# Sink-window attention and a SoLU layer on one core: the probabilities of chunks 8 to 22 turned by block DMAs through DRAM and 32x32 transposes on VectorE, with all steps in a new order

## The chip, the core and the metric

The kernel runs on one core of a Trainium2 chip. The metric is the device time of one execution in microseconds (us). Engines are named as in the profile: PE (TensorE, with PEld for its weight loads), DVE (VectorE), ACT (ScalarE), POOL (GpSimd) and SP (SyncE, which issues all DMAs here).

## The reference

Causal attention with a window of 128 positions and 4 sink positions that every query sees, for 4 batches of 8 heads, 768 positions and 64 columns a head. Its output goes, token by token, through a layer of 512 to 1024 to 512 columns with a SoLU and a layer norm between the two matrices.

```python
def _attn_ref(q, k, v, n_sink, window):          # 4 x 8 x 768 x 64
    scores = q @ k.T / sqrt(64)                  # kept where j < n_sink or 0 <= i - j < window
    a = exp(scores - max) / (sum + 1e-9)
    return a @ v

def _moe_ref(x, w_in, w_out, g_ln):              # x: 3072 x 512
    h = x @ w_in                                 # 512 -> 1024
    solu = h * softmax(h)
    ln = (solu - mean) / sqrt(var + 1e-6) * g_ln
    return ln @ w_out                            # 1024 -> 512
```

## The kernel before

The 3072 tokens are 24 chunks of 128 (4 batches of 6), numbered 0 to 23 in the order of work: 0 and 1 are the first blocks of batches 0 and 1, 2 to 6 and 7 to 11 the rest of these two batches, 12 to 17 batch 2, 18 to 23 batch 3. Chunks 12 and 18 are therefore first blocks of their batch.

A chunk passes these steps, each a small function of the kernel. `score` makes the scores of one head by two matmuls (L640, L641) into one of two PSUM banks. A bank holds the keys of this block and of the block before; `pick` (DVE, L647) chooses at each column whichever of the two is inside the window. `mask` (DVE, L658) adds the mask, takes the row maximum and frees the bank. `exps` (ACT, L669) makes exponentials and their sums, `invert` (DVE) the reciprocal of a sum, `normalise` (POOL, L680) multiplies, for half of the heads (`hb` is 0 or 1, four heads each). The probabilities `sc` stand with queries on partitions, and the product with v wants keys there. `turn_p` (PE, L687) transposes the four heads of a half into a PSUM tile `ptp`, and `take_p` (ACT, L691) copies this to `pt` in SBUF. `part_new` and `part_old` (POOL, L696, L702) split `pt` into keys of this block and of the one before, by the triangle. The sink columns go another way (`sinks_hi`, `sinks_lo`, `turn_sinks`, tiles `sk`, `skp`, `skt`). `value` (PE, L740, L751) multiplies by v into `av`: this is the PV step. Then `hidden` (PE, L771) makes 1024 columns `h` with three matmuls for one product (high and low halves), the SoLU and the norm follow on DVE, ACT and POOL, and for chunks 2 to 21 the result `u` is turned without PE: `store_u` writes it to DRAM (`ud`, L818), four `load_u` read it back with its 32-row blocks moved (`ub`, L823), and `flip_u` (DVE, L828) transposes each 32x32 block. `project` (PE, L858) multiplies by the second matrix into `o`, again three matmuls for one product, and `store` writes the output.

Every engine runs its instructions in order. The order is written out by hand: `ORDER` is a list of step numbers, and the kernel calls the steps one after another as it says. Tiles come from pools with few buffers: two banks for scores, three buffers for `sc`, three for `pt`, three for the tag `u` (which `u` and `ub` share), two for the tag `ob` (the output tile).

Of the kernel before, what the change touches and what calls it, by code (L numbers as in the profile page):

```python
# [19 lines left out]
    345, 0, 142, 2, 4, 143, 5, 243, 12, 347, 349, 59, 68, 6, 50, 350, 352, 7, 41, 23, 8, 146, 153, 244, 351, 145, 154,  # L20
    247, 3, 9, 147, 60, 254, 61, 62, 10, 155, 165, 181, 69, 161, 177, 70, 166, 182, 344, 156, 255, 164, 186, 180, 86,
    51, 71, 162, 178, 184, 163, 179, 72, 159, 185, 160, 52, 53, 54, 11, 74, 32, 24, 448, 42, 175, 176, 353, 183, 63,
    14, 25, 188, 26, 73, 75, 246, 76, 77, 65, 100, 157, 248, 348, 43, 56, 27, 190, 355, 93, 44, 45, 87, 64, 357, 66,
    144, 262, 278, 67, 29, 88, 107, 263, 279, 33, 89, 34, 35, 47, 28, 30, 261, 31, 277, 356, 360, 359, 452, 15, 55,
    57, 192, 36, 38, 90, 449, 16, 58, 17, 18, 267, 358, 187, 78, 459, 128, 283, 79, 80, 46, 48, 285, 189, 260, 276,
    49, 363, 101, 37, 94, 39, 81, 284, 354, 264, 135, 371, 102, 121, 40, 280, 191, 95, 20, 288, 96, 266, 282, 97, 19,
    194, 245, 103, 193, 21, 114, 104, 108, 265, 281, 109, 22, 207, 290, 83, 208, 82, 84, 1, 379, 464, 209, 552, 98,
    85, 256, 292, 364, 110, 111, 99, 129, 130, 287, 294, 131, 361, 286, 289, 214, 215, 216, 372, 450, 369, 380, 460,
    377, 136, 137, 210, 258, 112, 211, 386, 212, 362, 365, 370, 138, 378, 385, 291, 217, 346, 115, 373, 657, 381, 213,
    293, 218, 462, 366, 374, 389, 295, 382, 368, 376, 384, 391, 219, 308, 451, 309, 453, 454, 393, 220, 367, 310, 311,  # L30
    312, 315, 375, 461, 316, 387, 317, 456, 458, 91, 383, 388, 463, 455, 401, 457, 556, 139, 116, 390, 405, 760, 470,
    656, 403, 222, 117, 313, 395, 563, 478, 314, 761, 392, 553, 394, 402, 404, 92, 118, 397, 223, 406, 486, 465, 119,
    228, 407, 469, 399, 762, 473, 396, 398, 318, 408, 477, 481, 485, 319, 140, 105, 467, 471, 400, 409, 479, 320, 475,
    487, 483, 132, 410, 227, 321, 564, 411, 472, 226, 480, 225, 555, 412, 229, 113, 558, 557, 488, 230, 491, 560, 559,
    492, 416, 417, 468, 106, 413, 414, 122, 494, 123, 466, 415, 554, 474, 323, 231, 562, 482, 561, 565, 566, 257, 496,
    506, 418, 476, 322, 419, 489, 498, 484, 124, 567, 500, 764, 490, 125, 660, 667, 233, 126, 866, 120, 493, 495, 141,
    232, 505, 864, 234, 575, 235, 507, 236, 771, 583, 508, 497, 499, 237, 501, 867, 420, 329, 510, 591, 324, 569, 503,
    511, 328, 326, 571, 577, 502, 327, 512, 585, 330, 421, 579, 573, 587, 865, 127, 422, 504, 513, 668, 238, 514, 581,
    515, 589, 133, 134, 659, 520, 521, 221, 224, 332, 662, 661, 669, 663, 671, 331, 664, 516, 517, 576, 666, 518, 424,
    584, 425, 592, 570, 665, 670, 574, 334, 578, 582, 586, 590, 595, 239, 572, 240, 1078, 596, 580, 588, 519, 1086,  # L40
    423, 1087, 594, 427, 598, 593, 430, 333, 428, 600, 675, 522, 610, 683, 691, 241, 674, 682, 676, 684, 690, 523,
    602, 612, 597, 599, 429, 604, 692, 679, 687, 335, 609, 606, 695, 763, 524, 677, 608, 601, 685, 336, 765, 693, 611,
    337, 658, 767, 673, 681, 614, 615, 603, 605, 607, 1088, 431, 338, 698, 766, 768, 339, 325, 689, 616, 871, 868,
    525, 678, 680, 686, 694, 688, 697, 773, 527, 617, 770, 772, 775, 769, 526, 699, 618, 340, 341, 433, 619, 624, 774,
    528, 696, 700, 531, 701, 703, 620, 342, 621, 435, 780, 713, 702, 704, 432, 434, 436, 788, 625, 869, 796, 626, 779,
    787, 795, 714, 1089, 870, 532, 705, 715, 706, 778, 786, 622, 716, 718, 874, 707, 709, 708, 426, 627, 777, 623,
    711, 794, 719, 535, 533, 785, 793, 802, 710, 628, 1180, 529, 782, 790, 798, 781, 789, 712, 801, 720, 721, 629,
    797, 630, 438, 784, 722, 783, 437, 534, 882, 1189, 242, 439, 440, 872, 873, 883, 884, 441, 723, 724, 632, 635,
    975, 875, 728, 729, 730, 791, 799, 886, 877, 1188, 879, 631, 977, 792, 800, 442, 979, 443, 876, 537, 1190, 931,
    804, 981, 1191, 805, 803, 636, 731, 633, 888, 725, 536, 726, 806, 807, 896, 817, 1192, 885, 538, 727, 808, 444,  # L50
    878, 880, 819, 904, 637, 445, 818, 890, 889, 638, 1282, 446, 540, 639, 820, 809, 810, 811, 976, 812, 822, 897,
    898, 906, 814, 542, 813, 543, 544, 891, 815, 823, 545, 905, 824, 1384, 887, 732, 912, 816, 825, 539, 541, 733,
    899, 907, 546, 343, 826, 1382, 734, 895, 903, 1179, 1076, 827, 911, 915, 892, 900, 978, 917, 894, 547, 984, 735,
    828, 986, 548, 919, 641, 736, 737, 902, 910, 908, 739, 893, 832, 829, 640, 985, 927, 901, 992, 909, 914, 980, 833,
    982, 830, 913, 916, 987, 740, 1385, 831, 642, 742, 990, 918, 998, 643, 1181, 834, 835, 530, 743, 920, 922, 1000,
    644, 646, 647, 836, 447, 1006, 645, 837, 991, 999, 928, 921, 1383, 1007, 549, 550, 634, 924, 929, 648, 838, 930,
    649, 926, 1008, 932, 989, 933, 997, 923, 1005, 840, 843, 925, 650, 741, 1013, 993, 1001, 1009, 934, 935, 1077,
    1014, 1017, 1080, 651, 1082, 1290, 1084, 936, 995, 652, 1003, 1019, 1029, 841, 839, 994, 1011, 1002, 1010, 996,
    1004, 847, 937, 1079, 653, 1081, 1021, 1023, 1090, 845, 551, 1031, 1015, 938, 1183, 1012, 846, 1281, 942, 943,
    738, 744, 844, 1025, 1016, 1018, 1083, 1095, 1096, 1104, 1103, 1389, 1111, 944, 654, 746, 748, 1020, 974, 945,  # L60
    849, 1030, 1032, 1280, 1291, 1292, 1112, 1185, 1117, 1027, 939, 940, 941, 1098, 1022, 946, 1034, 1035, 947, 1097,
    1106, 1114, 1392, 750, 751, 1105, 1387, 1024, 1026, 745, 752, 753, 1113, 1092, 1036, 948, 747, 749, 1028, 1037,
    1100, 950, 1108, 951, 754, 1094, 1093, 953, 13, 1038, 1101, 1118, 848, 1039, 755, 851, 756, 757, 850, 1388, 1040,
    1041, 1293, 955, 852, 949, 1042, 1102, 1109, 758, 842, 1120, 1091, 1182, 1184, 1186, 1110, 1494, 1386, 854, 855,
    1099, 1107, 1195, 1203, 1211, 1283, 1285, 952, 1196, 1115, 1044, 1116, 956, 954, 1204, 1212, 1119, 1121, 1131,
# [90 lines left out]
P = 128  # L156
# [56 lines left out]
def _banded(ctx, tc, q, k, v, n_sink, window, w_in, w_out, g_ln, out, val, wts, wpool, consts):  # L213
# [660 lines left out]
    def loads(n):  # L874
        b, c = place(n)
        return 1 if turned(n) else 4 * (c == (b < EARLY))
# [194 lines left out]
```

## Time and profile before

| | us |
|---|---|
| runs, median of 3 (lowest to highest) | 452.35 (451.55 to 452.65) |
| the profiled execution | 452.25 |
| its span, first to last instruction | 450.3 |
| PE busy | 431.2 |
| PEld (weight loads) busy | 348.1 |
| DVE busy | 349.4 |
| ACT busy | 330.6 |
| POOL busy | 238.8 |

Busy time of an engine is the union of its instructions; weight loads overlap with matmuls. Of PE the granted clock was full (1.00, the upper of its two levels, 2.4 GHz) in all stretches but the last few us. A page lists a matmul as longer than the distance to the next, because matmuls are pipelined; how fast PE goes is read from the starts.

### The profile page before, as it was taken

Reading aid. Unit: us, or ns where it says so; the run is one execution under the profiler, and the core shown is the slowest. Engines: PE = TensorE matmul, PEld = TensorE weight load, DVE = VectorE, ACT = ScalarE, POOL = GpSimd, SP = SyncE. Lnnn points to the kernel's source line nnn. Section 1 sums busy time; section 2 is a strip of 40 time slices with the busy share of each in tenths; the row PEclk is TensorE's granted clock in tenths of the full one; section 3 lists DMA queues with packets and bytes.
Section 4 is the critical chain, followed back from the end, with each engine's and each line's share of the span. In section 5 each row is a group of like instructions: output and inputs, shape, how many; then the busy total and the mean of one; then the engine's idle time right before and its main releaser. Section 6 shows DMA issues by size and latency. Waiting matters only on the chain.

```text
span 450.3 us, 8541 instructions
## 1 busy us (share of the span) xinstructions
PE 431.2 (96%) x2631; PEld 348.1 (77%) x2631; DVE 349.4 (78%) x998; ACT 330.6 (73%) x843; POOL 238.8 (53%) x369
## 2 busy tenths in 40 slices
PE   4979899999999999999999999999999999999995
PEld 3536677888888788888888888877878878888884
DVE  2999999887997897887978797786878787767140
ACT  5989898888858865888797787686687865665442
POOL 7742455668667562667635775465536266344200
PEclk9999999999999999999999999999999999999999
DMA  8999287999899899635569997946815324242001
GB/s 226 280 342 265 47 165 107 127 175 183 209 155 166 203 183 176 176 95 144 118 174 175 192 165 141 172 143 166 199 26 186 117 71 146 90 141 70 25 26 52
DMA packets 142759, 67.74 MB, mean 150 GB/s; under 512 B 118956, under 2 KB 129460, under 8 KB 142708
## 3 DMA queue, kind: packets, MB, share of 16 engines
q1 hardware_dynamic: 142708, 67.13, 67.2%
q8 instruction: 23, 0.38, 0.4%
q14 instruction: 28, 0.23, 0.2%
HBM read 38.80 MB, written 16.91 MB: 124 GB/s over the span
## 4 chain that ended last, share of the span: by engine, by line
PE 65%; DVE 15%; ACT 7%; issue 4%; POOL 3%; DMA 3%; SPq 2%; POOLq 0%; DVEq 0%; ACTq 0%
PE o L858 25%; PE h L771 20%; PE av L751 6%; PE bank L640 4%; PE bank L641 3%; PE ptp L687 3%; DVE wbits L418 2%; DVE wbits L413 2%; ACT sc L669 2%; POOL sc L680 2%; DVE sc L658 2%; DMA ub<-ud 1%; PE av L740 1%; DMA wraw<-in_moe_w_in_dram 1%; DVE wbits L409 1%
## 5 line engine op out<-in xcount | busy, mean ns | idle before, releaser
L680 POOL TENSOR_TENSOR sc<-sc,rs 128x544 f32<-128x544 f32 (+1 forms) x48 | 55.9, 1166 | 95.7 <-DVE rs L675 76.5
L669 ACT ACTIVATE sc<-sc,nmx 128x136 f32<-128x136 f32 (+1 forms) x192 | 76.3, 400 | 16.9 <-DVE nmx L658 16.4
L858 PE MATMUL o<-w2h,uh 128*128 128x512 f32 (+1 forms) x200 | 81.2, 406 | 0.0
L609 POOL TENSOR_TENSOR ring<-kf,ring 64x512 fp32r<-64x512 f32 x48 | 65.7, 1370 | 27.7 <-ACT ring L604 21.0
L771 PE MATMUL h<-w1h,xh 128*128 128x512 f32 x192 | 77.3, 403 | 0.0
L858 PE MATMUL o<-w2h,ul 128*128 128x512 f32 (+1 forms) x200 | 77.0, 385 | 0.0
L858 PE MATMUL o<-w2l,uh 128*128 128x512 f32 (+1 forms) x200 | 77.0, 385 | 0.0
L771 PE MATMUL h<-w1h,xl 128*128 128x512 f32 x192 | 76.3, 397 | 0.1
L771 PE MATMUL h<-w1l,xh 128*128 128x512 f32 x192 | 75.8, 395 | 0.0
L658 DVE CUSTOM_DVE_ANT_0 sc<-bank,bias 128x136 f32<-128x136 f32 (+1 forms) x192 | 55.2, 294 | 11.1 <-PE bank L641 3.3
L640 PE MATMUL bank<-ring,qT 128*128 128x264 f32 (+1 forms) x176 | 51.6, 303 | 1.8 <-DVE nmx L658 1.6
L641 PE MATMUL bank<-ring,qX 128*128 128x264 f32 (+1 forms) x176 | 48.7, 283 | 0.0
L858 PEld LDWEIGHTS o<-w2h,ul 128*128 128x128 f32 x200 | 37.6, 188 | 8.6 <-DVE ul L846 0.5
L858 PEld LDWEIGHTS o<-w2h,uh 128*128 128x128 f32 x200 | 37.6, 188 | 8.6 <-issue 3.3
L771 PEld LDWEIGHTS h<-w1h,xl 128*128 128x128 f32 x192 | 36.0, 188 | 10.5 <-DVE xl L760 1.9
L691 ACT COPY pt<-ptp 128x512 f32<-128x512 f32 x48 | 27.5, 581 | 19.0 <-PE ptp L687 18.8
L640 PEld LDWEIGHTS bank<-ring,qT 128*128 128x128 f32 x176 | 33.1, 188 | 10.7 <-DVE nmx L658 4.8
L858 PEld LDWEIGHTS o<-w2l,uh 128*128 128x128 f32 x200 | 37.7, 189 | 4.5
L771 PEld LDWEIGHTS h<-w1h,xh 128*128 128x128 f32 x192 | 36.1, 188 | 5.7
L771 PEld LDWEIGHTS h<-w1l,xh 128*128 128x128 f32 x192 | 36.1, 188 | 5.5
L696 POOL TENSOR_SCALAR_AFFINE_SELECT pc<-pt 128x512 f32<-128x512 f32 x40 | 28.0, 701 | 21.7 <-ACT pt L691 21.5
L846 DVE TENSOR_TENSOR ul<-ur,uh 128x512 fp32r<-128x512 f32 x40 | 32.0, 802 | 8.0 <-ACT uh L842 8.0
(137 smaller groups left out, 976.4 us busy)
## 6 DMA issues: line engine op xcount, KB each, us to landing
qX<-qT SPq DMA_DIRECT2D x88, 128.0 KB, 2.6
ud<-u SPq DMA_DIRECT2D x20, 512.0 KB, 3.2
ub<-ud SPq DMA_DIRECT2D x80, 128.0 KB, 2.8
vn<-in_v_dram SPq DMA_DIRECT2D x24, 256.0 KB, 4.9
out_dram<-ob SPq DMA_DIRECT2D x23, 256.0 KB, 2.8
kn<-in_k_dram SPq DMA_DIRECT2D x12, 384.0 KB, 5.4
qn<-in_q_dram SPq DMA_DIRECT2D x12, 384.0 KB, 6.0
wraw<-in_moe_w_in_dram SPq DMA_DIRECT2D x8, 512.0 KB, 6.1
```

The source lines that it names most:

```text
L609: nc.gpsimd.tensor_tensor(t[ROWS[1 - x]], src[ROWS[x]], t[ROWS[x]].bitcast(F32), op=ALU.subtract)
L640: nc.tensor.matmul(o, st["qT", n, x][:, r, :], rhs, start=True, stop=False)
L641: nc.tensor.matmul(o, st["qX", n, x][:, r, :], rhs, start=False, stop=True)
L658: nc.vector.tensor_tensor_reduce(out=st["sc", n, hb][:, j, c0:c1], in0=st["s", n, h].rearrange("p a x -> p (a x)")[:, c0:c1], in1=bias0 if ...
L669: nc.scalar.activation(sc[:, i, c0:c1], sc[:, i, c0:c1], AF.Exp, bias=nmx[:, i:i + 1], scale=-1.0, accum_out=ssum[:, i:i + 1])
L680: nc.gpsimd.tensor_tensor(sc[:, :, c0:c1], sc[:, :, c0:c1], rs.unsqueeze(2).to_broadcast([P, HB, c1 - c0]), op=ALU.mult)
L691: nc.scalar.copy(pt, st["ptp", n, hb])
L696: nc.gpsimd.affine_select(pc, st["pt", n, hb], pattern=[[0, HB], [1, P]], compare_op=ALU.is_ge, fill=0.0, base=0, channel_multiplier=-1)
L751: nc.tensor.matmul(acc[ROWS[x], r, :], vals[:, 2 * r + x, :], p[:, 2 * jp + x, :], start=alone, stop=alone or (r, i) == (NPAIR - 1, 1))
L771: nc.tensor.matmul(st["h", n][:, cols], a[:, kt, :], w[:, kt, cols], start=(kt == 0 and m == 0), stop=(kt == KT1 - 1 and m == 2))
L846: nc.vector.tensor_tensor(ul, st["utp", n, g4], st["uh", n, g4].bitcast(F32), op=ALU.subtract)
L858: nc.tensor.matmul(st["o", n, i], a[:, kt % 4, :], part(w, kt)[:, i * wide:(i + 1) * wide], start=(kt == 0 and m == 0), stop=(kt == KT2 - ...
```

## The change

For chunks 8 to 22, without the first blocks 12 and 18, `turn_p` and `take_p` are gone. `normalise` writes the probabilities (without sink columns) to a new tile `pn`, in an order with the 32-column group outermost, and normalises the sink columns in place with a second, small instruction. `store_p` writes a half to a DRAM tile `pd`; four `load_p` read it back so that each block of 32 rows lies on the partitions of its 32 columns (`pb`); `flip_p` transposes the 32x32 blocks on DVE into `pt`. From `pt` on all is as before. `pn` takes buffers of the tag `ob`, and `pb` buffers of the tag `u`. `ORDER` is a new list for the whole kernel. Two names in the diff are set elsewhere: `HB` is 4 (heads a half), `SEG` 132 (columns of a block in a bank: 4 sink columns and 128 keys).

```diff
+FIRST_P, LAST_P = 8, 22
 ORDER = (
-    345, 0, 142, 2, 4, 143, 5, 243, 12, 347, 349, 59, 68, ...
+    344, 0, 12, 4, 142, 2, 345, 5, 143, 59, 348, 68, 32, ...
+    def carried(n):
+        return FIRST_P <= n <= LAST_P and place(n)[1] > 0
     def normalise(n, hb):
         c0, c1 = cols_of(place(n)[1])
         sc, rs = st["sc", n, hb], st["rs", n, hb]
-        nc.gpsimd.tensor_tensor(sc[:, :, c0:c1], sc[:, :, c0:c1], rs.unsqueeze(2).to_broadcast([P, HB, c1 - c0]),
-                                op=ALU.mult)
+        if not carried(n):
+            nc.gpsimd.tensor_tensor(sc[:, :, c0:c1], sc[:, :, c0:c1], rs.unsqueeze(2).to_broadcast([P, HB, c1 - c0]),
+                                    op=ALU.mult)
+            return
+        pn = st["pn", n, hb] = sb.tile([P, 4, HB, 32], F32, tag="ob", name=f"pn_{n}_{hb}", bufs=2)
+        nc.gpsimd.tensor_tensor(pn.rearrange("p g h f -> p h g f"),
+                                sc[:, :, 4:SEG].rearrange("p h (g f) -> p h g f", f=32),
+                                rs.unsqueeze(2).unsqueeze(3).to_broadcast([P, HB, 4, 32]), op=ALU.mult)
+        sv = sc.rearrange("p h (g s) -> p h g s", s=4)[:, :, 0:SEG // 4 + 1:SEG // 4, :]
+        nc.gpsimd.tensor_tensor(sv, sv, rs.unsqueeze(2).unsqueeze(3).to_broadcast([P, HB, 2, 4]), op=ALU.mult)
+
+    def store_p(n, hb):
+        if ("pd", n) not in st:
+            st["pd", n] = dr.tile([P, H * P], F32, tag="pd", name=f"pd_{n}", bufs=4)
+        wide = HB * 32
+        nc.sync.dma_start(st["pd", n].rearrange("p (g x) -> p g x", g=4)[:, :, hb * wide:(hb + 1) * wide],
+                          st["pn", n, hb].rearrange("p g h f -> p g (h f)"))
+
+    def load_p(n, g):
+        if ("pb", n) not in st:
+            st["pb", n] = sb.tile([P, 4, H * 32], F32, tag="u", name=f"pb_{n}", bufs=3)
+        nc.sync.dma_start(st["pb", n][32 * g:32 * (g + 1)],
+                          st["pd", n].rearrange("(c t) (g x) -> g t c x", c=4, g=4)[g])
+
+    def flip_p(n, hb):
+        pt = st["pt", n, hb] = sb.tile([P, HB, P], F32, tag="pt", name=f"pt_{n}_{hb}", bufs=3)
+        nc.vector.transpose(pt.rearrange("p h (c t) -> p h c t", c=4),
+                            st["pb", n].rearrange("p c (h f) -> p h c f", f=32)[:, hb * HB:(hb + 1) * HB])
...
+    def kept(k):
+        return lambda n: 0 if carried(n) else k
+
+    def carries(k):
+        return lambda n: k if carried(n) else 0
...
-        rest_k: 2, ring_sinks: 1, score: H, pick: H, mask: H, exps: NPAIR, invert: NHB, normalise: NHB, turn_p: NHB,
-        take_p: NHB, part_new: NHB, ...
+        rest_k: 2, ring_sinks: 1, score: H, pick: H, mask: H, exps: NPAIR, invert: NHB, normalise: NHB, turn_p: kept(NHB),
+        take_p: kept(NHB), store_p: carries(NHB), load_p: carries(4), flip_p: carries(NHB), part_new: NHB, ...
```

What the new order does is seen at three places. PE, before, near the end of the middle part: `bank` is a score bank, `o_18` the accumulator of chunk 18's projection, `ptp_21_1` the PSUM tile of the second half of chunk 21.

```order
L640 MATMUL bank_1_90<-ring_126,qT_22_0_4731 128x264
L641 MATMUL bank_1_90<-ring_126,qX_22_0_4793 128x264
L858 MATMUL o_18_0_4893<-w2h_0_484,uh_18_0_4760 128x512
L858 MATMUL o_18_0_4893<-w2l_0_485,uh_18_0_4760 128x512
L858 MATMUL o_18_0_4893<-w2h_0_484,ul_18_0_4772 128x512
L687 MATMUL ptp_21_1_4903<-ident_91,sc_21_1_4802 128x128 x4
L858 MATMUL o_18_0_4893<-w2h_0_484,uh_18_0_4760 128x512
L858 MATMUL o_18_0_4893<-w2l_0_485,uh_18_0_4760 128x512
L858 MATMUL o_18_0_4893<-w2h_0_484,ul_18_0_4772 128x512
```

PE in the changed kernel, where the sink columns of the same chunk 21 are turned (`skp_21`), between triplets of chunk 20's hidden layer:

```order
L643 MATMUL bank_0_89<-ring_126,qT_22_0_4575 128x264
L644 MATMUL bank_0_89<-ring_126,qX_22_0_4694 128x264
L803 MATMUL h_20_4856<-w1h_62,xh_20_4798 128x512
L803 MATMUL h_20_4856<-w1l_63,xh_20_4798 128x512
L803 MATMUL h_20_4856<-w1h_62,xl_20_4827 128x512
L755 MATMUL skp_21_4899<-ident_r_96,sk_21_4840 128x128
L803 MATMUL h_20_4856<-w1h_62,xh_20_4798 128x512
L803 MATMUL h_20_4856<-w1l_63,xh_20_4798 128x512
L803 MATMUL h_20_4856<-w1h_62,xl_20_4827 128x512
```

The two groups of four transposes of a chunk stand no more among PE's matmuls; only the sink columns are turned there.

DVE, before, at the second half of chunk 10's scores (`sc_10_1`; the ISA rows are `mask`):

```order
L550 STREAM_TRANSPOSE qf_12_2446<-qn_2_2055 128x512
L647 COPY_PREDICATED bank_0_89<-m_cur_115,bank_0_89 128x128
L647 COPY_PREDICATED bank_1_90<-m_cur_115,bank_1_90 128x128
L658 ISA sc_10_1_2428,nmx_10_1_2429<-bank_1_90,bias2_114 128x136
L658 ISA nmx_10_1_2429 128x1
L658 ISA sc_10_1_2428,nmx_10_1_2429<-bank_0_89,bias2_114 128x136
L658 ISA nmx_10_1_2429 128x1
```

DVE in the changed kernel, at the same scores:

```order
L650 COPY_PREDICATED bank_1_90<-m_cur_115,bank_1_90 128x128
L661 ISA sc_10_1_2291,nmx_10_1_2292<-bank_1_90,bias2_114 128x136
L661 ISA nmx_10_1_2292 128x1
L712 STREAM_TRANSPOSE pt_9_0_2366<-pb_9_2288 128x512
L712 STREAM_TRANSPOSE pt_9_1_2378<-pb_9_2288 128x512
L650 COPY_PREDICATED bank_0_89<-m_cur_115,bank_0_89 128x128
L661 ISA sc_10_1_2291,nmx_10_1_2292<-bank_0_89,bias2_114 128x136
L661 ISA nmx_10_1_2292 128x1
```

The two flips of chunk 9, which need the four loads of `pb_9`, now stand between the release of bank 1 and that of bank 0.

SP, before, at chunk 10's swaps of q halves (`qX`; PE's scores read them):

```order
L593 DMA qX_10_0_2085<-qT_10_0_1835 64x512
L594 DMA qX_10_0_2085<-qT_10_0_1835 64x512
L509 DMA qn_2_2055<-in_q_dram 32x96x32
L818 DMA ud_7_2188<-u_7_2149 128x1024
L509 DMA qn_2_2055<-in_q_dram 32x96x32
L823 DMA ub_7_2230<-ud_7_2188 32x4x256
L593 DMA qX_10_1_2256<-qT_10_1_2253 64x512
L594 DMA qX_10_1_2256<-qT_10_1_2253 64x512
```

SP in the changed kernel, at the same swaps and behind them:

```order
L701 DMA pd_9_2192<-pn_9_0_2138 512x1x128
L512 DMA qn_2_1967<-in_q_dram 32x96x32
L596 DMA qX_10_1_2228<-qT_10_1_2144 64x512
L597 DMA qX_10_1_2228<-qT_10_1_2144 64x512
L701 DMA pd_9_2192<-pn_9_1_2225 512x1x128
L901 DMA out_0_dram<-ob_4_0_2163 128x512
L850 DMA ud_7_2254<-u_7_2247 128x1024
L707 DMA pb_9_2288<-pd_9_2192 32x4x256
L596 DMA qX_11_0_2295<-qT_11_0_2270 64x512
L597 DMA qX_11_0_2295<-qT_11_0_2270 64x512
L707 DMA pb_9_2288<-pd_9_2192 32x4x256 x3
```

The stores of a chunk's two halves and its four loads stand between the swaps and the loads of q; the swap of chunk 11 stands behind the first load of `pb_9`, which waits for the stores.

## Rows read from the trace of the kernel before

**Rows 1.** The page's first part: busy us of each engine, share, instructions.

```profile
PE 431.2 (96%) x2631; PEld 348.1 (77%) x2631; DVE 349.4 (78%) x998; ACT 330.6 (73%) x843; POOL 238.8 (53%) x369
```

**Rows 2.** Stages: busy PE, PEld, DVE, ACT, POOL; PEclk, DMA share, GB/s.

```profile
0.00:60.00 60.00, 48.18 (x216) 32.10 (x217) 49.93 (x132) 48.86 (x122) 31.78 (x58) 1.00 0.81 230
60.00:150.00 90.00, 89.31 (x578) 73.69 (x579) 79.75 (x229) 73.69 (x187) 59.43 (x85) 1.00 0.98 161
150.00:400.00 250.00, 248.92 (x1563) 204.87 (x1564) 200.48 (x595) 185.16 (x488) 137.48 (x208) 1.00 0.64 148
```

**Rows 3.** Timeline of PE, the place in the order: start, us, instruction.

```profile
378.55 0.28 PE L640 MATMUL bank<-ring,qT 128*128 128x264 f32 x1
...
378.79 0.29 PE L640 MATMUL bank<-ring,qT 128*128 128x264 f32 x1
...
379.28 0.40 PE L858 MATMUL o<-w2l,uh 128*128 128x512 f32 x1
379.51 0.40 PE L858 MATMUL o<-w2h,ul 128*128 128x512 f32 x1
379.75 0.60 PE L687 MATMUL ptp<-ident,sc 128*128 128x128 f32 x4
380.11 0.48 PE L858 MATMUL o<-w2h,uh 128*128 128x512 f32 x1
380.42 0.39 PE L858 MATMUL o<-w2l,uh 128*128 128x512 f32 x1
```

**Rows 4.** Stage, instructions on `ptp` alone: PE, PEld, ACT; then the same.

```profile
150.00:400.00 250.00, 17.82 (x120) 14.29 (x120) 17.31 (x30) 1.00 0.64 148
```

**Rows 5.** Groups by line and form: busy us, mean ns; idle before.

```profile
L691 ACT COPY pt<-ptp 128x512 f32<-128x512 f32 x48 | 27.5, 581 | 19.0 <-PE ptp L687 18.8
...
L828 DVE STREAM_TRANSPOSE ur<-ub 128x512 f32<-128x512 f32 x40 | 27.9, 700 | 0.4 <-issue 0.3
...
L718 POOL TENSOR_TENSOR sk<-sc,sk 128x32 fp32r<-128x32 f32 x40 | 12.1, 310 | 16.7 <-ACT sk L711 16.2
...
L680 POOL TENSOR_TENSOR sc<-sc,rs 128x544 f32<-128x544 f32 x40 | 46.6, 1166 | 72.7 <-DVE rs L675 57.2 <-ACT ring L604 4.3 <-ACT sc L669 3.4
...
L647 DVE COPY_PREDICATED bank<-m_cur,bank 128x128 f32<-128x128 int32 x88 | 24.9, 288 | 7.6 <-PE bank L641 7.0
...
L658 DVE CUSTOM_DVE_ANT_0 sc<-bank,bias 128x136 f32<-128x136 f32 x160 | 46.5, 296 | 7.5 <-POOL sk L718 1.1
...
L669 ACT ACTIVATE sc<-sc,nmx 128x136 f32<-128x136 f32 x160 | 63.8, 401 | 15.3 <-DVE nmx L658 14.9
...
L669 ACT ACTIVATION_READ_ACCUMULATOR sc<-sc,nmx 128x1 f32 x192 | 36.3, 189 | 0.0
...
L696 POOL TENSOR_SCALAR_AFFINE_SELECT pc<-pt 128x512 f32<-128x512 f32 x40 | 28.0, 701 | 21.7 <-ACT pt L691 21.5
```

**Rows 6.** DMA issues: count, KB each, median us to landing.

```profile
ud<-u SPq DMA_DIRECT2D x20, 512.0 KB, 3.2
...
vn<-in_v_dram SPq DMA_DIRECT2D x24, 256.0 KB, 4.9
```

**Rows 7.** Tile `ub`: issue ns min/median/max, first and last start; landing.

```profile
L823 SPq DMA_DIRECT2D ub<-ud x80: 303/430/3316, 92.1 to 405.7; - x80
...
DMA to landing us min/median/max: 2.4/2.8/6.9
```

**Rows 8.** Waits of the DMA queue: us in total, times, longest.

```profile
SPq L823 <- DMA ud<-u: 38.3, 16, 4.2
```

**Rows 9.** Stretches of 10 us, columns as in the stages.

```profile
110.00:120.00 10.00, 10.00 (x73) 8.29 (x73) 9.56 (x26) 8.40 (x18) 6.15 (x13) 1.00 1.13 195
120.00:130.00 10.00, 9.86 (x50) 8.09 (x49) 9.75 (x24) 6.38 (x20) 8.09 (x10) 1.00 0.56 157
160.00:170.00 10.00, 10.00 (x76) 8.38 (x75) 8.95 (x28) 7.01 (x15) 6.76 (x12) 1.00 1.36 182
```

**Rows 10.** Waits of DVE from 150 to 400 us: us in total, times, longest.

```profile
DVE bank L647 <- PE bank L641: 9.9, 15, 2.0
```

## What I expected

> **What bounds the kernel now.** I read the page's busy shares first: TensorE (PE) is busy 431.2 us of a 450.3 us span, VectorE (DVE) 349.4, ScalarE (ACT) 330.6, GpSimd (POOL) 238.8 [rows 1]. A mean over stages can mislead, so the table by stage comes next: from 60 to 150 us PE is busy 89.31 of 90 us and from 150 to 400 us 248.92 of 250, so all its waiting there is 1.8 us [rows 2]. Busy time alone does not prove that PE has no room, since a pipelined matmul is listed as longer than the step to the next. The starts decide that [rows 3]: two 512-column matmuls follow each other by 0.23 to 0.24 us (379.28, 379.51, 379.75), so a triplet costs 0.70 us; a pair of score matmuls costs 0.24 (378.55 to 378.79); there is no hole between. In this middle part the time is the sum of PE's steps. The first 60 us (PE busy 48.18) have other limits. The change does not touch what is turned there: of the 192 transposes into `ptp`, 120 lie between 150 and 400 us [rows 4], eight each of the 15 chunks 8 to 22.
>
> In the Trainium skill, "Perfetto Trace Analysis", section "Identifying the Most-Contended Engine", matmul busy time is called a bad measure of TensorE's headroom and weight-load time a good one. By that rule PE would have 18% to spare in the middle (204.87 us of weight loads in 250), and rival 3 would be likelier than I make it; the starts disagree.
>
> **What it removes.** Chunks 8 to 22 without 12 and 18, which open a batch, are 13 chunks of two halves: 26 groups of four transposes. One group's price is read from the starts [rows 3]: the four take 379.75 to 380.11, 0.36 us, and the matmul behind them needs 0.31 to its successor where 0.235 is usual. Together 0.435 us; 26 x 0.435 = **11.3 us**, all in the middle, where PE has no other cover for it. On ACT 26 copies out of PSUM go, 26 x 0.581 = 15.1 us [rows 5], at an engine with 185 of 250 us busy [rows 2]: worth nothing by itself.
>
> **What it adds.** (a) DVE: 26 transposes of 128x512. The trace has that instruction at 0.700 us [rows 5]: 18.2 us. (b) POOL: normalising becomes two instructions. The small one is nearest to the 128x32 subtraction at 0.310 us [rows 5], 26 x 0.31 = 8.1 us; the big one now writes runs of 32, which the trace does not show for this operation. I keep 1.166 us (its old row), with half as much again, 1.75, as the far end. POOL has 137 of 250 us busy, so both matter only for the length of the turn. (c) SyncE and the DMA engines: per chunk two stores of 256 KB in 512-byte pieces and four loads of 128 KB. The loads have the shape of the `ub` loads: 0.43 us to issue, 2.8 us to landing in the median, 2.4 at least, 6.9 at most [rows 7]. The stores lie between a `ud` store (512 KB in long pieces, 3.2 us) and a `vn` load (256 KB in short pieces, 4.9 us) [rows 6]; I take 3.2, since direction and target are the same, and keep 4.9. SyncE issues 78 more DMAs (34 us) and stands 13 more times before a load until its store has landed; 16 such waits took 38.3 us [rows 8], so some 31 us more. That is 65 us on a queue that runs in order. Queued behind such a wait are the q swaps, `ub` loads and output stores, as the SyncE piece of the order shows; PE's scores wait for the swaps.
>
> **The turn itself becomes longer.** From the last score of a chunk to its PV step: pick 0.29, mask 0.30, two exponentials of 0.401 + 0.189, normalise 1.17, splitting in two 0.701 twice [rows 5], and about 1 us for the division and the hand-overs (my estimate): 5.3 us common to both. Before, four transposes and a copy add 0.435 + 0.581: 6.4 us. Now a store 3.2, three more issues 1.3, the last landing 2.8 and one transpose 0.70 add 8.0: **13.3 us**. Does PE have that much to do meanwhile? I counted, in the orders of both kernels, its steps between those two points, at 0.70 a triplet, 0.24 a score pair and 0.435 a turn [rows 3] (PV and sink steps left out, so it is counted low). Before it was 8.4 us (chunk 22) to 14.7 (chunk 14). Now it is 14.3 (22), 14.5 (21), 15.9 (8) to 22.0 (13). The new order pays for the longer turn with a longer lead, and the slack over the need stays about the same: 1.0 to 8.7 us against 2.0 to 8.3. With the store at 4.9 us or the normalising at its far end, chunks 21 and 22 are short by less than 1 us and the others are not. Chunks 8 and 9 share the DMA engines with loads of q in short pieces: the DMA share there is 1.36, against 0.64 in the middle [rows 2, 9].
>
> **What is late next: DVE's queue.** From 150 to 400 us DVE has 200.48 busy of 250 us [rows 2]. With 18.2 more it is 218.7 of 238.7: 92%, and its idle time must shrink from 49.5 to 20 us. A flip that waits for its load holds up the masks behind it; the DVE piece of the order shows the release of a score bank right behind two flips, and PE has two such banks. Can DVE run so full? From 110 to 130 us it did: 9.56 and 9.75 of 10 us, with PE at 10.00 and 9.86 [rows 9]. And the longest of its waits in the middle is for PE's own scores, 9.9 us [rows 10]; that part goes when PE gets faster.
>
> **Sum.** Span 450.3 - 11.3 = 439.0 us. New waits on PE: between none and the 8.7 us of rival 2 I take 2.7, 0.2 us for each of 13 turns, nearest to the row of now: 1.8 us of waiting over some 20 chunks, with a slack of the same size [rows 2]. Span 441.7; the profiled run took 452.25 us for a span of 450.3, so 1.95 lie outside, and the median of the runs is 0.1 above it: **443.7 us**. The first 60 us are re-ordered too and nothing is removed there; PE's idle 11.8 us in them [rows 2] can move either way, and I keep 1 us for that.
>
> **Rivals.**
> 1. *DVE becomes the bound (slower).* Its 49.5 us of idle time in the middle are waits of an in-order queue. If they all stay, because masks and flips wait as often as before, the middle takes 200.48 + 18.2 + 49.5 = 268 us, 18 more than 250: 470 us. It decides once idle stays above 31.3 us; with 37 of the 49.5 left the middle is 255.7 and the time 458. For it: 92% where the mean was 80%. Against it: 97% over the 20 us of [rows 9]. The Trainium skill sides with it ("VectorE: DVE Perf Modes", "Rules for kernel authors"): a 128x128 transpose belongs on TensorE if its result may lie in PSUM, and a DVE transpose is best within 32x32. A group of four heads costs 0.435 us on PE and 0.70 on DVE here, so the trace agrees on the engine time; it does not say which engine is short.
> 2. *Turns come late where the DMA engines are full.* Stores and loads of chunks 8 to 11 stand behind q loads, and `ub` landings came as late as 6.9 us [rows 7]. Two landings each 2.5 us late over a slack of 2.6 to 6 us cost 1.5 us in each of these four chunks, and 0.3 in the nine others: 8.7 us. Of the gain 2.6 us stay: 449.7.
> 3. *PE has headroom after all*, so what is removed was hidden: 452, no change. Against it speak the starts in [rows 3]; only places where PE waits anyway would hide it, and those add up to 1.8 us.
> 4. *All of it and a better start*: no new waits, and 1 us from the head: 440.
>
> **Chances.** Forecast (441 to 447): 0.58. Rival 1 (around 458): 0.12. Rival 2 (447 to 452): 0.17, of which 0.13 are still a gain that can be measured. Rival 3: 0.05. Rival 4: 0.08. A measurement of this kernel tells some 0.3% (1.4 us) from no change, so faster means below 451.0: 0.58 + 0.13 + 0.08 = 0.79; same 0.04 + 0.05 = 0.09; slower 0.12. The range leaves out rivals 1 and 3 and a little at either end: 440.3 to 451.0.
>
> **What would show it.** Right: PE's busy time 11 us smaller at the same spacing of 0.235 us; PE idle from 60 us to the last chunks below 5 us; DVE at 90% or more in the middle with its flips at 0.70 us; 22 copies on ACT in place of 48. Rival 1 shows as PE waiting for masks while DVE is busy throughout or stands at a flip. Rival 2 shows as landings of the new loads well over 3 us, with DVE waiting at the flips of chunks 8 to 11. The prediction is wrong if PE's idle time after the first 60 us grows by more than 6 us, or if the first 60 us change by more than 2.

## The result and the profile after

The changed kernel takes **448.06 us** (median of 6 runs, 446.73 to 449.33) against 452.50 for the kernel before (6 runs, 451.55 to 453.09): ratio 0.9897, interval 0.9883 to 0.9911. It is faster by 4.4 us and inside the range; 8.8 were forecast, and the time misses the forecast's own band of 441 to 447. Its profiled execution took 448.04 us for a span of 446.3.

The page's first part (engines, busy us, share, instructions) and the stages, columns as in [rows 1] and [rows 2]:

```profile
PE 421.2 (94%) x2527; PEld 336.3 (75%) x2527; DVE 364.6 (82%) x1024; ACT 317.4 (71%) x817; POOL 241.9 (54%) x395
```

```profile
0.00:60.00 60.00, 46.84 (x214) 31.66 (x215) 48.06 (x133) 48.45 (x121) 31.46 (x58) 0.97 0.81 225
60.00:150.00 90.00, 86.37 (x559) 69.65 (x559) 82.25 (x228) 74.31 (x193) 57.97 (x84) 1.00 1.02 169
150.00:400.00 250.00, 247.25 (x1504) 200.93 (x1504) 217.54 (x632) 173.41 (x462) 143.19 (x234) 1.00 0.86 201
```

PE's busy time fell by 10.0 us (431.2 to 421.2), so the work did leave PE. Its idle time in the span rose by 6.0, from 19.1 to 25.1 us, and the stages say where: 11.8 to 13.2 in the first 60 us, 0.7 to 3.6 from 60 to 150, 1.1 to 2.75 from 150 to 400. More than two thirds of the new idle time lies ahead of 150 us.

Groups by line and form (busy us, mean ns; then idle before): the new instructions cost what the rows before said.

```profile
L691 POOL TENSOR_TENSOR pn<-sc,rs 128x512 f32<-128x512 f32 x26 | 29.5, 1136 | 40.1 <-ACT sc L672 19.8 <-DVE rs L678 9.5 <-ACT qT L579 3.5
...
L712 DVE STREAM_TRANSPOSE pt<-pb 128x512 f32<-128x512 f32 x26 | 17.6, 693 | 0.0
...
L695 POOL TENSOR_TENSOR sc<-sc,rs 128x32 f32<-128x32 f32 x26 | 8.5, 326 | 0.0
```

DMA issues (count, KB each, median us to landing), and the `pd` stores (issue ns min/median/max, first and last start in us):

```profile
pd<-pn SPq DMA_DIRECT2D x26, 256.0 KB, 3.0
pb<-pd SPq DMA_DIRECT2D x52, 128.0 KB, 2.9
```

```profile
L701 SPq DMA_DIRECT2D pd<-pn x26: 553/561/2730, 152.3 to 388.2; - x26
```

The first store is issued at 152.3 us. Before that moment nothing is turned through DRAM, and only the order differs.

**The new waits from 60 to 150 us.** Waits of PE in this stage (total, times, longest); together 3.4 us, where before had 0.9:

```profile
PE bank L643 <- DVE nmx L661: 1.2, 2, 0.8
PE ptp L719 <- POOL sc L687: 0.8, 1, 0.8
PE bank L548 <- DVE nmx L661: 0.7, 1, 0.7
PE o L890 <- DVE w2l L453: 0.4, 1, 0.4
PE bank L643 <- POOL ring L612: 0.3, 1, 0.3
```

One of them closely: PE's timeline at 62.8 us, then DVE's (start us, us, instruction).

```profile
62.77 0.65 PE L548 MATMUL bank<-ident,qn 128*128 128x128 f32 x4 [0.73 <-DVE nmx L661]
```

```profile
60.67 0.67 DVE L412 TENSOR_SCALAR wbits<-wbits 128x512 int32<-128x512 int32 x1
61.26 0.65 DVE L540 SCALAR_TENSOR_TENSOR vsink<-vsraw,even,vsink 128x64 fp32r<-128x64 f32 x1
61.83 0.67 DVE L540 SCALAR_TENSOR_TENSOR vsink<-vsraw,odd,vsink 128x64 fp32r<-128x64 f32 x1
62.42 0.28 DVE L661 CUSTOM_DVE_ANT_0 sc<-bank,bias 128x136 f32<-128x136 f32 x1
```

The bank that PE needs is freed by a mask of chunk 3, and the mask stands behind some 2 us of preparation of weights and sink values. Before, the two `vsink` instructions stood ahead of all eight masks of that chunk; now they stand between the second and the third. DVE has no room to make up for it there: it is busy 9.91 of 10 us from 60 to 70 us and 9.79 from 70 to 80 (9.90 and 9.26 before).

**The clock.** Stretches (columns as in the stages) and PE's timeline around them:

```profile
24.00:28.00 4.00, 1.28 (x6) 0.70 (x5) 3.93 (x9) 2.98 (x6) 3.23 (x5) 1.00 1.16 310
28.00:32.00 4.00, 3.62 (x11) 1.56 (x9) 3.48 (x13) 1.30 (x3) 1.39 (x1) 0.58 1.04 272
```

```profile
23.20 1.04 PE L432 MATMUL ws<-wbits,minus 128*128 128x512 f32 x2
...
27.46 0.77 PE L641 MATMUL bank<-kf,qf 64*128 64x128 f32 x4 [2.64 <-DVE nmx L661]
28.16 2.08 PE L432 MATMUL ws<-wbits,minus 128*128 128x512 f32 x2
```

PE waited 2.64 us for a mask, and for some 3.4 us behind that it was granted its lower level, 1.2 GHz: the same two matmuls are listed with 1.04 us ahead of it and 2.08 in it. In the profiled execution of the kernel before there was no such stretch but at the very end. Its other executions are not all like that: of the 62 beside the experiments, 24 had a mean clock of 0.997 or more and took 452.7 us in the median, and 24 had 0.993 or less and took 453.0.

### The profile page after: what moved, and what is told of

It reads as the page before. It is cut to its first block, busy times and chain, and to the rows that moved or that the text cites. A ratio compares the mean times of both kernels' runs of the same rounds, so it can differ in the third digit from the quotient of the medians.

```text
span 446.3 us, 8537 instructions
## 1 busy us (share of the span) xinstructions
PE 421.2 (94%) x2527; PEld 336.3 (75%) x2527; DVE 364.6 (82%) x1024; ACT 317.4 (71%) x817; POOL 241.9 (54%) x395
## 4 chain that ended last, share of the span: by engine, by line
PE 58%; DVE 19%; DMA 6%; POOL 5%; issue 5%; ACT 5%; SPq 1%; DVEq 0%; POOLq 0%; ACTq 0%
PE o L890 23%; PE h L803 17%; PE av L783 6%; PE bank L643 3%; PE bank L644 3%; DVE qT L587 3%; DVE wbits L416 2%; DVE sc L661 2%; DMA kn<-in_k_dram 2%; DVE bank L650 2%; DMA wraw<-in_moe_w_in_dram 2%; POOL ring L612 2%; DVE u L818 1%; PE av L772 1%; DVE wbits L421 1%
## 5 line engine op out<-in xcount | busy, mean ns | idle before, releaser
L890 PE MATMUL o<-w2h,uh 128*128 128x512 f32 (+1 forms) x200 | 80.1, 401 | 0.0
L661 DVE CUSTOM_DVE_ANT_0 sc<-bank,bias 128x136 f32<-128x136 f32 (+1 forms) x192 | 54.0, 291 | 7.7 <-PE bank L644 1.7
L691 POOL TENSOR_TENSOR pn<-sc,rs 128x512 f32<-128x512 f32 x26 | 29.5, 1136 | 40.1 <-ACT sc L672 19.8
L687 POOL TENSOR_TENSOR sc<-sc,rs 128x544 f32<-128x544 f32 (+1 forms) x22 | 25.5, 1165 | 39.9 <-DVE rs L678 27.7
L813 ACT ACTIVATE e<-h,nm 128x1024 f32<-128x1024 f32 x24 | 26.8, 1115 | 16.3 <-DVE nm L808 13.9
```

What stands on the lines that cost most here:

```text
L661: nc.vector.tensor_tensor_reduce(out=st["sc", n, hb][:, j, c0:c1], in0=st["s", n, h].rearrange("p a x -> p (a x)")[:, c0:c1], in1=bias0 if ...
L687: nc.gpsimd.tensor_tensor(sc[:, :, c0:c1], sc[:, :, c0:c1], rs.unsqueeze(2).to_broadcast([P, HB, c1 - c0]), op=ALU.mult)
L691: nc.gpsimd.tensor_tensor(pn.rearrange("p g h f -> p h g f"), sc[:, :, 4:SEG].rearrange("p h (g f) -> p h g f", f=32), rs.unsqueeze(2).uns ...
L813: nc.scalar.activation(e, st["h", n], AF.Exp, bias=st["nm", n], scale=1.0, accum_out=se)
L890: nc.tensor.matmul(st["o", n, i], a[:, kt % 4, :], part(w, kt)[:, i * wide:(i + 1) * wide], start=(kt == 0 and m == 0), stop=(kt == KT2 - ...
```

## Experiments

Theory A: the missing gain is lost in the new order of 60 to 150 us. Theory B: it is lost by the turns themselves (L: they land late; D: DVE's queue is too full for the flips). Theory C: by the clock in the first 60 us. In the diffs, BEFORE and CHANGED are the two lists of steps. Intervals are of the ratio to the kernel before, which took 452.8 to 453.2 us in these batches.

### The two halves of the order

```diff
-ORDER = CHANGED
+ORDER = BEFORE[:814] + [s for s in CHANGED if s not in BEFORE[:814]]
```

> The changed kernel, but with the order of the kernel before up to chunk 7's turn (some 135 us of the trace); from there the changed order, and all 13 chunks turned through DRAM. Theory A (of the 11.3 us that PE was freed of, some 4 were lost between 60 and 150 us because the new order of that part makes PE wait for masks and for POOL's normalising, although no chunk is turned through DRAM there): about 444 us, with PE's waits from 60 to 130 us as in the kernel before. Theory B (the loss comes from the turns themselves, late landings and a full DVE queue): 448 us as before, the waits only move to later. Theory C (the lower granted clock in the first 60 us, 0.97, costs it): 446 to 447, with the clock back at 1.00.

Measured: 449.27 us, 0.9911 (0.9890 to 0.9931). PE's idle time from 60 to 130 us fell from 2.9 us in the changed kernel to 1.1, and around the seam, from 140 to 165 us, 3.1 us of new waits came, for masks (1.5), `sk` (0.9) and others.

```diff
-ORDER = CHANGED
+ORDER = BEFORE[:473] + [s for s in CHANGED if s not in BEFORE[:473]]
```

> As the kernel with the old order up to chunk 7, but the old order ends at some 80 us of the trace (chunk 3). Theory A: between, 445.5 to 446.5 us, since PE's waits at 62 to 79 us (about 3 us in the changed kernel) go and those at 90 to 150 stay. Theory B: 448. Theory C: the same time as the longer old head, 446 to 447, since the clock falls at 28 us only.

Measured: 461.70 us, 1.0177 (1.0152 to 1.0202). PE waited 12.1 us at once for a normalising behind the seam. This is far from all three theories; it shows what a bad seam costs.

```diff
-ORDER = CHANGED
+ORDER = CHANGED[:620] + [s for s in BEFORE if s not in CHANGED[:620]]
-        return FIRST_P <= n <= LAST_P and place(n)[1] > 0
+        return n in ()
```

> No chunk is turned through DRAM: the order of the changed kernel up to some 100 us of the trace, then that of the kernel before, all turns on PE. Theory A: 452.5 plus 2 to 4 us, 455, with the same PE waits at 62 to 91 us as in the changed kernel. Theory B: 452.5. Theory C: 453 to 454 with the lower clock in the first 60 us.

Measured: 457.56 us, 1.0096 (1.0069 to 1.0123), 4.5 us slower than before with nothing turned through DRAM. The stage from 60 to 150 us, and PE's waits in it:

```profile
60.00:150.00 90.00, 87.00 (x561) 70.56 (x560) 79.23 (x215) 71.21 (x183) 55.80 (x78) 1.00 0.96 157
```

```profile
PE ptp L717 <- POOL sc L685: 0.8, 1, 0.8
PE bank L546 <- DVE nmx L659: 0.7, 1, 0.7
PE bank L641 <- DVE nmx L659: 0.4, 1, 0.4
PE o L888 <- DVE w2l L451: 0.4, 1, 0.4
```

These are waits of the changed kernel with the same lengths; of its waits in this stage, the 0.8 us for a mask and the 0.3 for `ring` are missing here. PE's idle time in this stage is 3.0 us against 0.7 before. So 2.3 of the 2.9 us come with the order and not with the turns: this part of A holds. The half clock in the first 60 us lasted 6.8 us here; what it has of the 4.5 us this run doesn't tell.

```diff
-ORDER = CHANGED
+ORDER = BEFORE[:668] + [s for s in CHANGED if s not in BEFORE[:668]]
```

> The order of before up to 90 us (644 steps; only five of them stand on the other side of that point in the changed order), then the changed order; all 13 chunks are carried. Theory A (the missing gain sits in the new order of 60 to 150 us, where nothing is carried yet): PE's waits at 62.8, 71.8, 75.4 and 78.1 us (0.9 + 0.3 + 1.0 + 0.7 = 2.8 us) go, those at 90.6, 126.0 and 144.5 stay: 445.3 us. Rival (waiting only moves: what PE doesn't wait for here it waits for later, since DVE and POOL set the pace): 448, with new waits after 90 us. Rival clock: the half-clock stretch near 28 us stays in both and decides nothing.

Measured: 450.53 us, 0.9954 (0.9941 to 0.9967). PE at its longest wait:

```profile
121.60 1.09 PE L719 MATMUL ptp<-ident,sc 128*128 128x128 f32 x4 [4.89 <-POOL sc L687]
```

The waits at 62.8, 71.8 and 78 us went and this one came, 30 us behind the cut: PE stood 4.9 us at a turn whose normalising was not done.

```diff
-ORDER = CHANGED
+ORDER = BEFORE[:735] + [s for s in CHANGED if s not in BEFORE[:735]]
```

> As the one with the cut at 90 us, with the cut at 100 us (711 steps, some ten of them on the other side). Theory A: 444.7 us, the wait of 0.6 at 90.6 us goes too; more steps are out of place at the seam, which may give up to 1 us back. Rival (waiting only moves): 448.

Measured: 447.78 us, 0.9885 (0.9870 to 0.9900): the changed kernel's time. PE's long waits behind the cut:

```profile
128.69 0.28 PE L755 MATMUL skp<-ident_r,sk 128*128 128x128 f32 x1 [0.90 <-POOL sk L750]
...
146.74 0.36 PE L644 MATMUL bank<-ring,qX 128*128 128x264 f32 x1 [1.05 <-DMA qX<-qT]
156.39 0.39 PE L643 MATMUL bank<-ring,qT 128*128 128x264 f32 x1 [0.90 <-DVE nmx L661]
```

In this run PE is idle for 0.6 us from 60 to 118 us (2.6 in the changed kernel) and for 3.8 from 118 to 176 us (1.6). A's forecasts for the four mixed orders (444 to 446.5) all failed. The rival named for the last two, that waiting only moves (448), gave the time of this one.

C finds no support here: the profiled execution of this run had the full clock up to its last few us, and PE was busy for 421.5 us and idle for 25.1 in it, against 421.2 and 25.1 in the changed kernel. What a stretch at half clock can cost is seen against the first run (old order up to chunk 7), which has the same order far beyond 60 us. The same instruction, `skp` of chunk 2, in the first run (half clock from 25.6 to 29.0 us) and here (full clock):

```profile
61.35 0.28 PE L755 MATMUL skp<-ident_r,sk 128*128 128x128 f32 x1 [0.42 <-POOL sk L750]
```

```profile
59.66 0.28 PE L755 MATMUL skp<-ident_r,sk 128*128 128x128 f32 x1 [0.43 <-POOL sk L750]
```

In this pair a stretch of 3.4 us at 1.2 GHz goes with 1.7 us. It isn't a fixed price: in the run with free loads below, which has the changed order, the half clock came from 12.9 to 19.7 us instead, 6.8 us long, and the instruction that stands at 62.77 us in the changed kernel stands at 62.36 there. Whether and where a stretch comes differs between runs of one order. In the 6 runs of the changed kernel the mean clock went from 0.990 to 0.997 and the time with it, 449.33 to 446.73.

### The turns

```diff
-        return FIRST_P <= n <= LAST_P and place(n)[1] > 0
+        return n in ()
-ORDER = CHANGED
+ORDER = [turn_p where store_p stood, take_p where flip_p stood] in CHANGED
```

> The changed kernel's order of all other steps, but the 26 halves are turned on PE again: transposes where the stores stood, copies on ACT where the flips stood; no store, no load, no flip. If freeing PE of 26 x 0.435 us is what the change gains, and its own waits (about 3 us at PV steps) go away with it: 448.1 + 11.3 - 3 = 456 us. If the gain comes from the new order and the removed transposes were hidden (rival 3 of the prediction): 448 to 450.

Measured: 471.24 us (467.88 to 477.47), 1.0391 (1.0309 to 1.0472). The page's first part, and PE's longest waits from 150 to 400 us:

```profile
PE 430.6 (92%) x2631; PEld 346.6 (74%) x2631; DVE 351.3 (75%) x998; ACT 330.1 (71%) x843; POOL 235.3 (50%) x369
```

```profile
PE ptp L716 <- POOL sc L684: 5.2, 5, 2.0
PE ptp L716 <- ACT pt L720: 3.2, 2, 2.9
```

With the turns back on PE the changed order is some 20 us slower (the profiled spans are 466.8 and 446.3 us). PE is busy 9.4 us more than in the changed kernel, and idle 11.1 us more (36.3 against 25.1), since in this order it reaches the turns before their data; five of the 26 stand 6 to 17 steps behind the place of their store. So the new order alone doesn't bring the gain, and rival 3 falls in that form. That PE has no room to hide a turn this run can't show, as PE stands idle so long in it.

```diff
+        src = [m for m in range(FIRST_P, n) if carried(m)]
         nc.sync.dma_start(st["pb", n][32 * g:32 * (g + 1)],
-                          st["pd", n].rearrange("(c t) (g x) -> g t c x", c=4, g=4)[g])
+                          st["pd", src[-1] if src else n].rearrange("(c t) (g x) -> g t c x", c=4, g=4)[g])
```

> The changed order; each of the 52 loads reads the DRAM tile of the carried chunk before its own, which is long written, so that a load waits for no store (the probabilities are those of another chunk). Same instructions, same traffic. Theory L (the turn is too long at some chunks: PE's waits at PV steps, 2.5 us in 150 to 400 us, are late landings): they go, 445.6 us. Rival D (the flips are late because DVE is full, not because data is): 448, PV waits unchanged. Rival A: 448 less what L has, with the waits of 60 to 150 us unchanged.

Measured: 447.38 us, 0.9896 (0.9870 to 0.9922): no difference. POOL and then PE at the longest wait of a PV step: in the changed kernel (chunk 15), and below that in this run.

```profile
280.78 0.65 POOL L728 TENSOR_SCALAR_AFFINE_SELECT pc<-pt 128x512 f32<-128x512 f32 x1 [0.74 <-DVE pt L712]
...
282.09 0.64 POOL L728 TENSOR_SCALAR_AFFINE_SELECT pc<-pt 128x512 f32<-128x512 f32 x1
282.81 1.29 POOL L612 TENSOR_TENSOR ring<-kf,ring 64x512 fp32r<-64x512 f32 x1
284.17 0.97 POOL L734 TENSOR_SCALAR_AFFINE_SELECT pt<-pt 128x512 f32<-128x512 f32 x1
```

```profile
285.20 0.44 PE L783 MATMUL av<-pt,vn 128*64 128x128 f32 x4 [0.51 <-POOL pt L734]
```

```profile
280.36 0.65 POOL L729 TENSOR_SCALAR_AFFINE_SELECT pc<-pt 128x512 f32<-128x512 f32 x1 [0.74 <-DVE pt L713]
...
282.38 1.29 POOL L612 TENSOR_TENSOR ring<-kf,ring 64x512 fp32r<-64x512 f32 x1
283.74 0.97 POOL L735 TENSOR_SCALAR_AFFINE_SELECT pt<-pt 128x512 f32<-128x512 f32 x1
```

```profile
284.77 0.44 PE L784 MATMUL av<-pt,vn 128*64 128x128 f32 x4 [0.52 <-POOL pt L735]
```

The wait stays although no load waits for its store. A 1.29 us write into `ring` stands on POOL between the third and the fourth part, and ahead of the first part POOL had stood 0.74 us for the flips. Each is longer than PE's wait of 0.5 us. The flips in turn waited for nothing on DVE: idle time before all 26 is 0.0 us in the row shown above, so their loads had always landed and their place in DVE's queue sets their time. L falls: late landings aren't it, late places in the queues are. Rival D's forecast for this run (448, the waits at PV steps unchanged) fits; the next run tries D.

```diff
-        nc.vector.transpose(pt.rearrange("p h (c t) -> p h c t", c=4),
-                            st["pb", n].rearrange("p c (h f) -> p h c f", f=32)[:, hb * HB:(hb + 1) * HB])
+        nc.scalar.copy(pt.rearrange("p h (c t) -> p h c t", c=4),
+                       st["pb", n].rearrange("p c (h f) -> p h c f", f=32)[:, hb * HB:(hb + 1) * HB])
```

> The changed order; the 26 flips are copies on ACT in the same place of the order (the blocks are not transposed, so the probabilities are wrong); DVE has 18.2 us less, ACT some 15 us more. Theory D (DVE's queue is too full: score banks are released late behind flips): the waits for row maxima after 165 us go (0.36 + 0.48 + 0.37) and with them the wait of 0.7 for u: 446 us. Theory L: PV waits stay as they are, 447.5 to 448.5. If ACT is in turn held up by copies that wait for loads, exponentials are late: 450 or more.

Measured: 450.78 us, 0.9950 (0.9932 to 0.9968), 2.7 us slower than the changed kernel. Its profiled execution took 451.67, 3.6 more than the changed kernel's. The first 45 us and the middle, then an instruction just behind the first 60 us:

```profile
0.00:45.00 45.00, 34.72 (x128) 21.98 (x129) 30.77 (x90) 32.60 (x75) 24.14 (x50) 0.89 0.92 267
...
150.00:400.00 250.00, 246.00 (x1493) 200.01 (x1493) 203.59 (x607) 186.60 (x493) 140.68 (x232) 1.00 0.86 202
```

```profile
65.51 0.66 PE L548 MATMUL bank<-ident,qn 128*128 128x128 f32 x4 [0.50 <-DVE nmx L661]
```

Up to here both kernels are the same, and this instruction comes at 65.51 in place of 62.77 us. Of the 3.6 us, 2.7 are there already, with the half clock lasting 13.6 us of the first 60 in place of 3.4; that the clock is their cause is the likely reading. From 150 to 400 us DVE has 14 us less to do than in the changed kernel, and PE's idle time there is 4.0 us in place of 2.75. The waits for masks fell from 0.7 to 0.5 us, where D had 1.2 go away; those for POOL at PV steps rose from 1.0 to 2.2. D falls as it was put: a freer DVE does not give PE its time back. What earlier flips would be worth stays open, as the copies stand in ACT's queue and the turns end hardly sooner after the last score (median 18.7 us, 19.3 in the changed kernel, counted as below).

### Fewer chunks, later

```diff
-        return FIRST_P <= n <= LAST_P and place(n)[1] > 0
+        return n in (16, 17, 19, 20, 21, 22)
-ORDER = CHANGED
+ORDER = BEFORE[:1689] + [s for s in CHANGED if s not in BEFORE[:1689]]
```

> The order of before up to 260 us, then the changed order; only chunks 16, 17 and 19 to 22 (six, 12 halves) are carried, the others are turned on PE. Theory A2 (the longer lead has to be built up once, by scores 2 to 16 us earlier in the order; the changed kernel builds it from 60 to 160 us, where DVE is 90 to 99% busy, and PE waits for it; later DVE has a fifth of its time free and it is cheap): before's 452.5 less 12 x 0.435 = 5.2, plus under 1 us at the seam: 447.3 to 448.3, as fast as the changed kernel with 13. Rival (each carried chunk nets only what it nets there, 4.4 / 13 = 0.34 us): 450.5. PE's waits from 60 to 250 us as in before in either case.

Measured: 453.77 us, 1.0014 (0.9996 to 1.0031). PE at its longest wait, and DVE ahead of it:

```profile
295.86 0.59 PE L642 MATMUL bank<-ring,qT 128*128 128x264 f32 x1 [6.46 <-DVE nmx L660]
```

```profile
288.63 0.08 DVE L660 DVE_READ_ACCUMULATOR2_ANT nmx<- 128x1 f32 x1
294.47 0.59 DVE L676 TENSOR_SCALAR rs<-ssum 128x4 f32<-128x4 f32 x1 [5.76 <-ACT sc L671]
```

DVE was not busy, it stood: the first of the two short instructions of `invert`, which needs the sums of exponentials, came to the head of its queue 5.76 us too early, and the mask that frees the bank stood behind it.

```diff
-        return FIRST_P <= n <= LAST_P and place(n)[1] > 0
+        return n in (13, 14, 15, 16, 17, 19, 20, 21, 22)
-ORDER = CHANGED
+ORDER = BEFORE[:1201] + [s for s in CHANGED if s not in BEFORE[:1201]]
```

> The same with the cut at 178 us; chunks 13 to 17 and 19 to 22 (nine, 18 halves) are carried. Theory A2: 452.5 - 18 x 0.435 = 444.7, plus 0 to 1.5 us at the seam and at PV steps: 444.7 to 446.2, faster than the changed kernel with 13. Rival (0.34 us a chunk): 449.4.

Measured: 451.54 us, 0.9970 (0.9953 to 0.9988). Two waits behind the seam:

```profile
205.61 0.66 PE L718 MATMUL ptp<-ident,sc 128*128 128x128 f32 x4 [1.00 <-POOL sc L686]
210.28 0.50 PE L802 MATMUL h<-w1h,xh 128*128 128x512 f32 x1 [2.87 <-ACT xh L787]
```

```diff
-        return FIRST_P <= n <= LAST_P and place(n)[1] > 0
+        return n in (9, 10, 11, 13, 14, 15, 16, 17, 19, 20, 21, 22)
-ORDER = CHANGED
+ORDER = BEFORE[:909] + [s for s in CHANGED if s not in BEFORE[:909]]
```

> The same with the cut at 129 us; chunks 9 to 11, 13 to 17 and 19 to 22 (twelve, 24 halves) are carried. Theory A2: 452.5 - 24 x 0.435 = 442.1, plus what building the lead between 130 and 170 us costs, where DVE is 87 to 92% busy: the order of before up to 135 us with all 13 showed 4.4 us of waits at its seam, so 444 to 447. Rival (0.34 us a chunk): 448.4.

Measured: 452.96 us, 1.0005 (0.9989 to 1.0021), with waits of 1.8, 1.2, 0.5 and 0.9 us between 158 and 173 us. (The 4.4 us at the seam in the expectation are 3.1 in the list of that run's waits.) A2 gave too short a time for all three, so it falls as it was put: that DVE has a fifth of its time free does not make a change of order cheap. The rival, too, is 2.1 to 4.6 us short (450.5, 449.4 and 448.4). What the rows show is single waits of 1 to 6.5 us; in the first run it is an in-order queue that met an instruction too early, in the other two what held up the releaser wasn't followed. Taken off, the 6.5 us of the first would leave 447.3, A2's number; that is worked out and not shown.

```diff
-ORDER = CHANGED
+ORDER = THIRD
```

> All 13 chunks are carried; the steps are those of the changed kernel, and up to some 55 us they stand as in before. Behind that is a third order: neighbouring steps of which neither needs the other have been exchanged, so that a PE instruction that waited stands later and what it waited for stands earlier. The last score of chunks 3 to 7 stands where before has it (within 3 us of PE's work, not 2 to 5 us earlier as in the changed kernel), and the lead of the turns is built up at chunks 8 and 9 (20 and 23 us from the last score to the PV step). Theory A3 (the missing 7 us are a price of the order alone, not of the turns, the loads or a full DVE): 452.5 - 26 x 0.435 = 441.2 us can be had with the same 26 turns through DRAM, and less where waits of before itself fall away too: 437 to 442. Rival F (a carried turn brings its own waiting: in five orders so far 6.5 to 10 us of the gain were missing, wherever it was put): 446 to 449 again, with PE's idle time after 60 us at 5 us or more.

Measured: 472.33 us, 1.0431 (1.0389 to 1.0474). Some of PE's longest waits:

```profile
PE bank L643 <- DVE nmx L661: 12.1, 11, 3.5
PE bank L644 <- DMA qX<-qT: 7.1, 2, 5.0
...
PE av L783 <- DMA vn<-in_v_dram: 2.4, 1, 2.4
```

The exchanges had moved DMA issues as freely as the rest, and swaps and loads came up to 5 us late. The waits for masks are the largest part; why the masks were late wasn't followed. The time is far above both forecasts, so the run decides neither for A3 nor for its rival.

## Why the prediction was right, and where not

**PE as the bound, and what is removed: right.** 11.3 us were to leave PE. Its busy time fell by 10.0; some of its work ran at half clock, which lists it longer, but the run with the old order to 100 us, with full clock up to its last few us, has 421.5 and not less. Rival 3 (no change) is refuted by the result: 10.0 us less busy, 6.0 more idle, 4.0 less span. The Trainium skill ("Perfetto Trace Analysis", "Identifying the Most-Contended Engine") would still read 80% from the weight loads in the middle (200.93 of 250 us); no run shows such headroom.

**The durations: right.** Flip 0.693 us (0.700 taken), big normalising 1.136 (1.166), small one 0.326 (0.31), store 3.0 us (3.2), load 2.9 (2.8). DVE in the middle rose by 17.1 us (18.2). What ACT's 26 copies were worth no run shows by itself. SyncE's waits for the stores were put too high: 8 of 2 us at most, 8.4 us in all, where I had 13 and 31 us.

**The length of a turn: wrong, with little harm.** Added up without queues it was 13.3 us. From the records of the 13 chunks, from the last score to the end of the last flip, it was 13.9 (chunk 22) to 23.1, in the median 19.3; before, by the same count to the end of the copy, 6.4 to 13.2 and 9.1. In chunk 15 the second half is normalised 5.8 us after the last score and its store has landed at 9.3. The last load is issued only at 12.8, since `ub` loads and swaps stand ahead of it, lands at 17.2, and the flips end at 19.3. So the slack of 1.0 to 8.7 us was gone: in 10 of 13 chunks the last part ends 0.2 to 2.2 us after the PV step has begun (4 of 13 before). Even so the stage of the turns has only 1.7 us more idle time on PE (2.7 were allowed), and at the longest of its PV waits, as the run with free loads shows, neither store nor load sets the time but places in DVE's and POOL's queues.

**DVE: right in amount, wrong as the next bound.** It was busy 217.5 of the 250 us, 87%; 92% were forecast, of a middle shorter by 11.3 us. Rival 1 did not come, and with 14 us less on DVE PE waits no less. The Trainium skill's rule ("VectorE: DVE Perf Modes", "Rules for kernel authors"), which leaves a 128x128 transpose to TensorE, agrees with the engine times here (0.36 us for four against 0.693) and not with the kernel's: the dearer engine had the room.

**Rival 2's time came, its cause did not.** The measured time lies in its band (447 to 452) and not in the forecast's, and it is inside the range only because the range takes in most of that band: for the size of the gain that is luck. Of the cause nothing is seen: the loads landed after 2.9 us in the median and 4.4 at most, DVE never stood before a flip, and with loads that wait for no store nothing changed.

**The start: the step that failed.** The prediction kept 1 us for the re-ordered first 60 us and nothing for 60 to 150, although the new order covers the whole kernel. PE's idle time grew by 1.3 us in the first 60 us, by 2.9 from 60 to 150 and by 1.7 from 150 to 400; only the last has the turns in it, and 2.7 were allowed for it. The account of the profiled executions: 10.0 us less busy and 6.0 more idle leave 4.0, and the span fell by 4.0. So the term that was put at nothing, waits between 60 and 150 us, is the largest loss. By its own test ("if the first 60 us change by more than 2") the start is undecided: 1.3 us are idle time, and what the 3.4 us at half clock cost there isn't settled, as the pairs of runs above differ. PE's idle time from 60 to 400 us is 6.4 us, not below 5 as "right" would have shown, and 4.6 more than before, below the 6 that "wrong" asked for. A row that should have warned me was there: DVE is busy 97% from 110 to 130 us [rows 9], and I read this as proof that it can run so full. At 62.8 us the other side is seen: on a DVE that is busy 9.91 of 10 us, instructions put ahead of a mask kept PE waiting.

**What stays open.** That 2.3 of the 2.9 us come with the order is shown, by the run with the new start and no turn. That they could be had back is not: with the old order to 100 us they went, and as much came behind it (4.4 us of idle time from 60 to 176 us, 4.2 in the changed kernel). Whether another order has the turns without such waits stays open: five orders with 12 or 13 carried chunks took 447.8 to 453 us, two more 462 and 472, and each lost part of the gain or all of it. How much of the start's loss is chance is not settled either, as half-clock stretches differ between runs of one order.

## What to carry to other kernels

When a change comes with a new order, price every stage that the order touches, also those where nothing is added or removed: here 4.3 of the 6.0 us of new idle time lie there. Taking a wait away at one place is no gain yet: in the mixed orders as much or more came behind the seam. Look at which instruction frees what the bound engine waits for, and what the new order puts ahead of it in that queue; a mean busy share does not show it, and an engine with 20% free time can still stand 6 us at an instruction that came too early. For a long detour like a turn through DRAM, add up the places in the queues and not only the transfers: they made 13 us into 19.

## What the runs showed of the hardware

TensorE's granted clock can go with a difference of a third or more of what the change brings: after 2.64 us of idle time it was at 1.2 GHz for 3.4 us; a stretch of the same length went with the same instruction of one order 1.7 us later, and 10.2 us more at half clock with 2.7. In these runs the place counted for more than the length: with 6.8 us of it from 12.9 to 19.7 us, the same instruction at 62 us came no later.

The DMA queues now move 81.4 MB in place of 67.7, and some transfers landed later: `qX` after 3.2 us in the median (2.6 before), `ub` after 3.3 (2.8), `ud` after 3.7 (3.2). The changed order with the turns on PE moves 67.7 MB, and has 2.9, 2.8 and 3.0: so what `ub` and `ud` lost goes with the traffic, and half of `qX` with the order. Others landed sooner, `vn` after 4.0 us (4.9 before), and that with either traffic.
